# Addition of epsilon to the softmax sums by GpSimd, not by ACT, from the second pair of heads on

## The chip, the cores and the metric

The kernel runs on one core of a Trainium2 chip. The metric is the device time of one execution in microseconds (us). The engines are named as the profile names them: PE (TensorE, matmuls and transposes; PEld its weight loads), DVE (VectorE), ACT (ScalarE), POOL (GpSimd) and SP (the queue that issues most DMAs). Each engine works through its own list of instructions in order, and an instruction that needs another engine's result waits at the head of its list, with all that stand behind it.

## The reference

Two batches of eight heads, 768 tokens, head dimension 64. Attention is allowed between a query and a key that fall to the same of 16 clusters; two dense layers follow, each w_in (512 to 2048) and w_out (2048 to 512), with an activation between.

```
scores = where(mask, q @ k.T / 8, -1e9)
scores = scores - max(scores, axis=-1)
attn = exp(scores)
attn = attn / (sum(attn, axis=-1) + 1e-9)
x = attn @ v                      # (2, 8, 768, 64), laid out as (1536, 512)
x = leaky(x @ w_in) @ w_out
out = rational(x @ w_in2) @ w_out2
```

The change concerns the `+ 1e-9`.

## The kernel before

The attention stage comes first and takes about a third of the time. Its work is cut into 96 **units**: 128 queries of one head against all 768 keys. Twelve units make a **head pair** (two heads), and there are eight head pairs. Two successive units, an even and an odd one, share one small tile `sum` (128 x 2) for their softmax sums; such a **couple** is normalized together. There are 48 couples. The two dense layers (`make_h`, L1097 for `h` and `y`) follow, and PE works there without a pause.

The order of instructions on each engine is that in which `run` writes them. Its loop over i has one step for each unit:

- DVE: `row_max(i)` (L592, the negated maximum `nm` over the scores of unit i in PSUM); in even steps `recip` (L615, the reciprocal of `sum` of the couple i-2, i-1); further down two subtractions `lo(i-4)` (L646, the low half `pl` of the transposed probabilities in `pT`); then what the preparation of later heads needs (`is_max` L357, `first` L365, `onehot` L372), and `merge_add` (L684, tile `xf`).
- POOL: in even steps `normalize` of the units i-2 and i-1 (L619, `e` times the reciprocal, 128 x 768 each); then `finish` (L702 and L703, which cut an attention result `xf` into a high half `xha`/`xhb` and a low half `xla`/`xlb`); then pieces of preparation in the slot "end": `vsplit` (L447, L448), `split_hi` and `split_lo` (L293, L298), `rank` (L362, which needs the result of `is_max` on DVE). Late in the stage it also cuts the first weights of the dense layer (L920, `wil`, which needs `wih` of ACT, L917).
- ACT: two casts `hi(i-4)` (L640, `ph`), copies for the preparation, `exp(i)` (L603, which also adds up the row into `sum`), and in odd steps `denom(i)` (L610, `sum` plus the constant in `eps`).
- PE: six transposes of unit i-4 (L627, into two `pT` tiles), the scores of unit i+1 (L583, `s`), and the product with the values (L663, `o`).

The PSUM tiles in which the transposes land rotate over three buffers (`pq`), shared with the transposes and similarities of the preparation. So a transpose can start when the tile three places before it has been read, for the most part by the subtraction L646. `denom`, `recip` and `normalize` of one couple are a chain: `exp` of the odd unit, the addition, the reciprocal, the two multiplications.

Of the kernel before, what the change touches and what calls it, by code (L numbers as in the profile page):

```python
# [13 lines left out]
AF = mybir.ActivationFunctionType  # L14
ALU = mybir.AluOpType
# [2 lines left out]

P = 128
BIG = float(2.0 ** 60)  # L20
LN_SHIFT = 63
SQRT_MAGIC = float(0x1FBD1DF5)
EXP_SCALE = 2.0 ** -112
# [7 lines left out]
def clustered_attention_moe_moe2(  # L31
# [14 lines left out]
    nc = tc.nc  # L46
# [30 lines left out]
    for c in range(C):  # L77
        nc.vector.memset(iom[:, :, c:c + 1], float(c - C))
    eps = const.tile([P, 1], F32, name="eps")
    nc.vector.memset(eps, 1e-9)  # L80
    lnb = const.tile([P, 1], F32, name="lnb")
    nc.vector.memset(lnb, -LN_SHIFT * math.log(2.0))
    lnc = const.tile([P, 1], F32, name="lnc")
    nc.vector.memset(lnc, 1.000001 * 2.0 ** -LN_SHIFT)
    av = const.tile([P, 4], F32, name="av")
# [48 lines left out]
    UP = HP * T  # L134
    NU = NPAIR * UP
# [6 lines left out]
    class Attention:  # L142
# [65 lines left out]
        def prep_pieces(self, p):  # L208
# [196 lines left out]
            def onehot_near_out(i, h):  # L405
                x = st["pp"].pop(("n", i))[D:KB, 0:S]
                y = st["b"][D:KB, i, h].rearrange("p t n -> p (t n)")
                if i == 0:
                    nc.scalar.activation(y, x, AF.Copy, scale=-BIG)
                else:  # L410
# [13 lines left out]
            def onehot_out(hs=ALL):  # L424
# [3 lines left out]
                for i in range(2):  # L428
                    nc.scalar.activation(
                        st["ot"][0:C * T, i, hs[0]:hs[1]],  # L430
                        pp[0:C * T, i, hs[0]:hs[1]], AF.Copy, scale=-BIG if i == 0 else 1.0,
                    )
# [171 lines left out]
                un["e"], un["s"][:, 0:S], AF.Exp, bias=un["nm"], accum_out=un["recip"]  # L604
            )

        def denom(self, u, alone=False):
            un = self.unit[u]
            x = un["recip"] if alone else un["sum"]
            nc.scalar.activation(x, x, AF.Identity, bias=eps)  # L610

        def recip(self, u, alone=False):
            un = self.unit[u]
# [162 lines left out]
        def run(self, extra, fill):  # L776
            TL = 4
            pieces = {}
            for p in range(NPAIR):
                for i, slot, f in self.prep_pieces(p):  # L780
                    pieces.setdefault(max(i, -1), {}).setdefault(slot, []).append(f)
            self.startup(*fill)
            first = -1
            last_prep = max(pieces)
            n_groups = NU // QT
            part = -(-2 * T // QT)
            for i in range(first, NU + TL + 11):
                def go(slot):
                    for f in pieces.get(i, {}).get(slot, []):
                        f()  # L790

                gi, r = divmod(i - TL - 3, QT)
                ok = 0 <= gi < n_groups
                live = 0 <= i - TL < NU
                go("dve0")
                if 0 <= i < NU:
                    self.row_max(i)
                if i == 1:
                    f0 = self.pair[0]["fn"]
                    f0["rank"]((1, 2), nc.vector)  # L800
                    f0["first"]((1, 2))
                    f0["onehot"](0, (1, 2))
                    f0["onehot"](1, (1, 2))
                if NU - 1 <= i <= NU:
                    self.recip(i - 1, True)
                    self.normalize(i - 1)
                elif i % 2 == 0 and 0 <= i - 2 < NU:
                    self.recip(i - 2)
                    self.normalize(i - 2)
                    self.normalize(i - 1)  # L810
                if live:
                    self.trans_p(i - TL, 0)
                    self.hi(i - TL, 0)
                    self.trans_p(i - TL, 1)
                    self.hi(i - TL, 1)
                if ok and r == QT - 1:
                    self.values(gi, part * r, 2 * T)
                    self.merge_copy(gi)
                go("act")
                if 0 <= i < NU:  # L820
                    self.exp(i)
                    if i >= NU - 2:
                        self.denom(i, True)
                    elif i % 2 == 1:
                        self.denom(i)
                if 0 <= i + 1 < NU:
                    self.scores(i + 1)
                go("pe")
                if ok and r < QT - 1:
                    self.values(gi, part * r, part * (r + 1))  # L830
                if live:
                    self.lo(i - TL, 0)
                    self.lo(i - TL, 1)
                go("pa")
                if ok and r == QT - 1:
                    self.merge_add(gi)
                go("dve")
                gd, rd = divmod(i - TL - 3 - 7, QT)
                if rd == 0 and 0 <= gd < n_groups:
                    self.finish(gd)  # L840
                go("end")
                if 0 <= i < TL:
                    self.warm(5)
                if i == UP:
                    fill[1].preload(4)
                if UP + 6 <= i < NU - 2 * UP and i % 3 == 0:
                    fill[1].step()
                if i == last_prep:
                    self.pc.close()
                    extra[0]()  # L850
                elif i > last_prep:
                    extra[1](i >= NU + TL)
# [167 lines left out]
    with tc.manual_schedule():  # L1020
# [60 lines left out]

        LNC = float(2.0 ** -LN_SHIFT)
        LAG = 3
# [246 lines left out]
```

## Time and profile before

| what | value |
|---|---|
| median of 3 runs | 793.15 us (792.27 to 793.41) |
| profiled execution, its own time | 793.16 us |
| its span, first to last instruction | 791.0 us |
| PE, PEld busy | 775.6 us (98%), 659.6 us (83%) |
| DVE, ACT, POOL busy | 646.7 us (82%), 510.6 us (65%), 387.7 us (49%) |
| chain that ended last | PE 85%, DVE 7%, ACT 3%, POOL 2% |

The shares are means over stages that differ. The attention stage runs from the start to about 262 us of the span. In it DVE, ACT and POOL are far busier than over the whole, and the small instructions that the change moves all lie in it.

### The profile page before, as it was taken

Reading aid. Unit: us, or ns where it says so; the run is one execution under the profiler, and the core shown is the slowest. Engines: PE = TensorE matmul, PEld = TensorE weight load, DVE = VectorE, ACT = ScalarE, POOL = GpSimd, SP = SyncE. Lnnn points to the kernel's source line nnn. Section 1 sums busy time; section 2 is a strip of 40 time slices with the busy share of each in tenths; the row PEclk is TensorE's granted clock in tenths of the full one; section 3 lists DMA queues with packets and bytes.
Section 4 is the critical chain, followed back from the end, with each engine's and each line's share of the span. In section 5 each row is a group of like instructions: output and inputs, shape, how many; then the busy total and the mean of one; then the engine's idle time right before and its main releaser. Section 6 shows DMA issues by size and latency. Waiting matters only on the chain.

```text
span 791.0 us, 11944 instructions
## 1 busy us (share of the span) xinstructions
PE 775.6 (98%) x4026; PEld 659.6 (83%) x4026; DVE 646.7 (82%) x1106; ACT 510.6 (65%) x1015; POOL 387.7 (49%) x400
## 2 busy tenths in 40 slices
PE   8899999999999999999999999999999999999997
PEld 6699999899878888888888888888888888888886
DVE  7888999998988678877577568759988888888896
ACT  5789998998899455454254346357766666666662
POOL 3787887877576324230031023267645545653341
PEclk9999999999999999999999999999999999999999
DMA  3594563662320334335445453530101001000012
GB/s 103 153 236 122 150 150 86 146 172 65 92 91 1 106 107 149 117 128 213 139 145 179 131 179 112 187 106 28 54 13 41 27 27 41 15 0 1 1 54 106
DMA packets 42109, 78.58 MB, mean 99 GB/s; under 512 B 5248, under 2 KB 25280, under 8 KB 42048
## 3 DMA queue, kind: packets, MB, share of 16 engines
q1 hardware_dynamic: 41760, 77.65, 32.5%
q8 instruction: 32, 0.52, 0.3%
q14 instruction: 29, 0.24, 0.1%
q10 hardware_dynamic: 288, 0.16, 0.1%
HBM read 49.84 MB, written 9.96 MB: 76 GB/s over the span
## 4 chain that ended last, share of the span: by engine, by line
PE 85%; DVE 7%; ACT 3%; POOL 2%; issue 1%; DMA 1%; DVEq 0%; SPq 0%; POOLq 0%; ACTq 0%
PE h L1097 32%; PE y L1097 31%; PE o L663 6%; PE s L583 6%; PE pT L627 6%; PE sims L326 2%; DVE pl L646 2%; DVE nm L592 2%; ACT ph L640 1%; PE pa L243 1%; POOL e L619 1%; ACT e L603 1%; DVE acc L1218 1%; DMA st<-in_moe_w_in_dram 1%; PE warm L722 1%
## 5 line engine op out<-in xcount | busy, mean ns | idle before, releaser
L646 DVE TENSOR_TENSOR pl<-pT,ph 128x384 fp32r<-128x384 f32 x192 | 97.2, 547 | 15.7 <-ACT ph L640 15.5
L619 POOL TENSOR_SCALAR e<-e,sum 128x768 f32<-128x768 f32 x96 | 87.5, 923 | 43.6 <-DVE sum L615 29.0
L920 POOL TENSOR_TENSOR wil<-wf,wih 128x512 fp32r<-128x512 f32 x32 | 42.8, 1350 | 128.3 <-ACT wih L917 116.7
L1130 ACT CAST gh<-h 128x512 fp32r<-128x512 f32 x96 | 56.4, 588 | 69.4 <-DVE h L1177 67.9
L1097 PE MATMUL h<-xha,wil 128*128 128x512 f32 x256 | 99.7, 390 | 0.0
L1097 PE MATMUL h<-xla,wih 128*128 128x512 f32 x256 | 99.7, 389 | 0.0
L1097 PE MATMUL h<-xha,wih 128*128 128x512 f32 x256 | 99.7, 389 | 0.0
L1150 POOL TENSOR_SCALAR z<-y,abv 128x512 f32<-128x512 f32 x48 | 37.0, 771 | 117.3 <-ACT y L1146 117.3
L1135 DVE TENSOR_TENSOR gl<-h,gh 128x512 fp32r<-128x512 f32 x96 | 65.6, 686 | 33.8 <-ACT gh L1130 33.5
L640 ACT CAST ph<-pT 128x384 fp32r<-128x384 f32 x192 | 82.2, 481 | 15.2 <-PE pT L627 13.4
L592 DVE TENSOR_REDUCE nm<-s 128x1 f32<-128x768 f32 x96 | 90.9, 947 | 0.5
L603 ACT ACTIVATE e<-s,nm 128x768 f32<-128x768 f32 x96 | 87.4, 910 | 5.7 <-DVE nm L592 3.5
L627 PE MATMUL pT<-ident,e 128*128 128x128 f32 x576 | 81.0, 275 | 1.9 <-DVE pl L646 1.8
L1218 DVE TENSOR_TENSOR acc<-y,acc 128x512 f32<-128x512 f32 x84 | 56.9, 691 | 29.8 <-PE y L1097 29.5
L910 DVE SCALAR_TENSOR_TENSOR wf<-st,wf 128x512 int32<-128x512 int32 x124 | 80.4, 702 | 0.0
L1097 PE MATMUL y<-gl,woh 128*128 128x512 f32 x192 | 74.9, 390 | 0.2 <-DVE gl L1135 0.2
L1097 PE MATMUL y<-gh,wol 128*128 128x512 f32 x192 | 74.8, 389 | 0.0
L1097 PE MATMUL y<-gh,woh 128*128 128x512 f32 x192 | 74.7, 389 | 0.0
L1097 PE MATMUL y<-woh,gl 128*128 128x512 f32 x191 | 74.5, 390 | 0.0
L1097 PE MATMUL y<-woh,gh 128*128 128x512 f32 x191 | 74.4, 390 | 0.0
L1097 PE MATMUL y<-wol,gh 128*128 128x512 f32 x191 | 74.4, 389 | 0.0
L627 PEld LDWEIGHTS pT<-ident,e 128*128 128x128 f32 x576 | 67.3, 143 | 7.5 <-DVE pl L646 2.1
(130 smaller groups left out, 1904.0 us busy)
## 6 DMA issues: line engine op xcount, KB each, us to landing
st<-in_moe_w_out_dram SPq DMA_DIRECT2D x32, 512.0 KB, 4.5
st<-in_moe_w_in_dram SPq DMA_DIRECT2D x30, 512.0 KB, 4.6
a<-hl SPq DMA_DIRECT2D x56, 192.0 KB, 4.0
b<-hl SPq DMA_DIRECT2D x28, 192.0 KB, 5.4
wf<-scratch_wi SPq DMA_DIRECT2D x14, 256.0 KB, 2.9
qraw<-in_q_dram SPq DMA_DIRECT2D x16, 192.0 KB, 3.3
kraw<-in_k_dram SPq DMA_DIRECT2D x16, 192.0 KB, 3.7
vraw<-in_v_dram SPq DMA_DIRECT2D x8, 384.0 KB, 5.1
```

The lines of the kernel that those rows point to most:

```text
L583: nc.tensor.matmul(s[:, n0:n1], lhsT=x[0:hi, 0, t, :], rhs=kk[:, n0:n1], start=m == 0, stop=m == 1,)
L592: nc.vector.reduce_max(un["nm"], un["s"][:, 0:S], axis=AX.X, negate=True)
L603: nc.scalar.activation(un["e"], un["s"][:, 0:S], AF.Exp, bias=un["nm"], accum_out=un["recip"])
L619: nc.gpsimd.tensor_scalar(un["e"], un["e"], un["recip"], 1.0, op0=ALU.mult, op1=ALU.mult)
L627: nc.tensor.transpose(pp[:, kt * P:(kt + 1) * P], un["e"][:, k0:k0 + P], ident)
L640: nc.scalar.copy(un["hi", part], un["pT", part])
L646: nc.vector.tensor_tensor(self.group[gi]["pl"][:, part * n:(part + 1) * n, i * P:(i + 1) * P], un["pT", part], f32(un["hi", part]), op=ALU ...
L910: nc.vector.scalar_tensor_tensor(wi, hold["st", i][:, :, :, 1 - w], sc, wi, op0=op, op1=ALU.bitwise_or)
L1097: nc.tensor.matmul(o, lhsT=l, rhs=r, start=(first and idx == 0), stop=(last and idx == n - 1),)
L1130: nc.scalar.copy(d["gh"], d["h"])
L1135: nc.vector.tensor_tensor(d["gl"], d["h"], f32(d["gh"]), op=ALU.subtract)
L1218: nc.vector.tensor_tensor(a, y, a, op=ALU.add)
```

## The change

For the couples of units 13 to 93 the addition of epsilon is done by POOL, at the end of the odd step, behind that step's "end" pieces. There are 41 such couples. The six couples of the first head pair keep ACT, as do the last two units, which are handled singly.

```
+EPS = 1e-9
...
-        def denom(self, u, alone=False):
+        def denom(self, u, alone=False, gp=False):
             un = self.unit[u]
             x = un["recip"] if alone else un["sum"]
-            nc.scalar.activation(x, x, AF.Identity, bias=eps)
+            if gp:
+                nc.gpsimd.tensor_scalar(x, x, EPS, 1.0, op0=ALU.add, op1=ALU.mult)
+            else:
+                nc.scalar.activation(x, x, AF.Identity, bias=eps)
...
                     if i >= NU - 2:
                         self.denom(i, True)
-                    elif i % 2 == 1:
+                    elif i % 2 == 1 and i < UP:
                         self.denom(i)
...
                 go("end")
+                if UP <= i < NU - 2 and i % 2 == 1:
+                    self.denom(i, gp=True)
```

Three places show the new order. The line numbers of the changed kernel are a few higher (L612 is the addition on POOL, L619 there the reciprocal, L623 the normalization).

POOL, the two couples at the turn of a head pair, before: `e` is the normalization of two units, `vs` is `vsplit`, `xha`/`xla` is `finish`, `sv` is `rank`.

```order
L619 TENSOR_SCALAR e<-e,sum 128x768 x2
L447 TENSOR_SCALAR vs<-vraw 128x6x64
L448 TENSOR_TENSOR vs<-vraw,vs 128x6x64
L702 TENSOR_SCALAR xha<-xf 128x384
L703 TENSOR_TENSOR xla<-xf,xha 128x384
L619 TENSOR_SCALAR e<-e,sum 128x768 x2
L447 TENSOR_SCALAR vs<-vraw 128x6x64
L448 TENSOR_TENSOR vs<-vraw,vs 128x6x64
L362 TENSOR_TENSOR sv<-sv,iom 128x384
```

The same place in the changed kernel:

```order
L623 TENSOR_SCALAR e<-e,sum 128x768 x2
L448 TENSOR_SCALAR vs<-vraw 128x6x64
L449 TENSOR_TENSOR vs<-vraw,vs 128x6x64
L706 TENSOR_SCALAR xha<-xf 128x384
L707 TENSOR_TENSOR xla<-xf,xha 128x384
L612 TENSOR_SCALAR sum<-sum 128x2
L623 TENSOR_SCALAR e<-e,sum 128x768 x2
L448 TENSOR_SCALAR vs<-vraw 128x6x64
L449 TENSOR_TENSOR vs<-vraw,vs 128x6x64
L363 TENSOR_TENSOR sv<-sv,iom 128x384
L612 TENSOR_SCALAR sum<-sum 128x2
```

The addition stands behind the pieces of the couple before it, and ahead of the normalization.

DVE around `rank`, with the semaphores waited for, before:

```order
L357 TENSOR_TENSOR sv<-sv,mx 128x384 [waits DVE_49]
L592 TENSOR_REDUCE nm<-s 128x1 [waits PE_49]
L615 RECIPROCAL sum<-sum 128x2 [waits Activation_49]
L646 TENSOR_TENSOR pl<-pT,ph 128x3x128 [waits Activation_49] x2
L365 TENSOR_REDUCE mx<-sv 128x24 [waits Pool_49]
```

The same place in the changed kernel:

```order
L358 TENSOR_TENSOR sv<-sv,mx 128x384 [waits DVE_49]
L593 TENSOR_REDUCE nm<-s 128x1 [waits PE_49]
L619 RECIPROCAL sum<-sum 128x2 [waits Pool_49]
L650 TENSOR_TENSOR pl<-pT,ph 128x3x128 [waits Activation_49] x2
L366 TENSOR_REDUCE mx<-sv 128x24 [waits DVE_49]
```

DVE's order stays; its reciprocal now waits for POOL, not for ACT. No other instruction of DVE, PE or SP changes its place.

ACT, the step of an odd unit and the next, before (`x` is a copy for the preparation, `tmp` one for the merge):

```order
L603 ACTIVATE e,sum<-s,nm 128x768
L610 ACTIVATE sum<-sum,eps 128x2
L640 CAST ph<-pT 128x3x128 x2
L246 ACTIVATE x<-pa 128x384
L603 ACTIVATE e,sum<-s,nm 128x768
```

And in the changed kernel:

```order
L604 ACTIVATE e,sum<-s,nm 128x768
L644 CAST ph<-pT 128x3x128 x2
L247 ACTIVATE x<-pa 128x384
L604 ACTIVATE e,sum<-s,nm 128x768
L644 CAST ph<-pT 128x3x128 x2
```

The addition between the exponential and the casts is gone.

## Rows read from the trace of the kernel before

**Rows 1.** Busy time by stretch: us from start, length, each engine, granted clock, DMA share, GB/s.

```profile
150.00:180.00 30.00, 29.82 (x210) 27.43 (x209) 28.93 (x54) 27.29 (x67) 23.92 (x28) 1.00 0.54 143
200.00:222.00 22.00, 21.07 (x139) 18.67 (x137) 20.89 (x40) 19.80 (x47) 13.00 (x17) 1.00 0.26 60
```

**Rows 2.** Chain by line, first for 150 to 180 us, then for 200 to 222 us.

```profile
by line: PE o L663 28.4%; PE pT L627 27.1%; PE s L583 26.3%; PE sims L326 8.4%; PE pa L243 4.4%; ACT ph L640 2.9%; PE po L418 1.6%; ACT sv L337 0.8%; issue 0.3%
...
by line: DVE pl L646 33.1%; DVE nm L592 30.7%; POOL e L619 8.1%; issue 5.9%; DVE xf L684 5.4%; DVE sv L357 3.6%; POOL xla L703 3.4%; DVE oh L372 2.8%; DVE sum L615 2.2%; POOL xlb L703 2.1%; DVE mx L365 2.1%; POOL xha L702 1.7%; POOL xhb L70
```

**Rows 3.** Line L610: ns min/median/max, and who waited for it (us, times).

```profile
L610 ACT ACTIVATE sum<-sum,eps x49: 294/296/298, 20.4 to 255.4; 128x2 f32<-128x2 f32 x47, 128x1 f32<-128x1 f32 x2
...
  DVE sum L615: 1.3, 3
```

**Rows 4.** Timeline of POOL (start us, length us), two small instructions.

```profile
0.24 0.10 POOL L1314 MEMSET const-float32-0.0<- 128x1 f32 x1 [0.24 <-issue]
...
192.13 0.30 POOL L702 TENSOR_SCALAR xhb<-xf 128x128 fp32r<-128x128 f32 x1
```

**Rows 5.** The page's group of the normalization: busy us, mean ns, idle before it, releaser.

```profile
L619 POOL TENSOR_SCALAR e<-e,sum 128x768 f32<-128x768 f32 x96 | 87.5, 923 | 43.6 <-DVE sum L615 29.0
```

**Rows 6.** Timelines of POOL and DVE: the last `finish` before five reciprocals, and these.

```profile
78.96 1.01 POOL L703 TENSOR_TENSOR xla<-xf,xha 128x384 fp32r<-128x384 f32 x1
79.95 0.15 DVE L615 RECIPROCAL sum<-sum 128x2 f32<-128x2 f32 x1
...
108.98 1.01 POOL L703 TENSOR_TENSOR xla<-xf,xha 128x384 fp32r<-128x384 f32 x1
109.63 0.16 DVE L615 RECIPROCAL sum<-sum 128x2 f32<-128x2 f32 x1
...
139.07 1.01 POOL L703 TENSOR_TENSOR xla<-xf,xha 128x384 fp32r<-128x384 f32 x1
139.31 0.15 DVE L615 RECIPROCAL sum<-sum 128x2 f32<-128x2 f32 x1
...
169.12 1.02 POOL L703 TENSOR_TENSOR xla<-xf,xha 128x384 fp32r<-128x384 f32 x1
169.39 0.16 DVE L615 RECIPROCAL sum<-sum 128x2 f32<-128x2 f32 x1
...
198.61 1.01 POOL L703 TENSOR_TENSOR xlb<-xf,xhb 128x384 fp32r<-128x384 f32 x1
199.43 0.16 DVE L615 RECIPROCAL sum<-sum 128x2 f32<-128x2 f32 x1
```

**Rows 7.** Timeline around one `rank`, the reciprocal and the normalization behind it.

```profile
203.63 1.01 POOL L362 TENSOR_TENSOR sv<-sv,iom 128x384 f32<-128x384 f32 x1 [0.49 <-DVE sv L357]
...
204.34 0.15 DVE L615 RECIPROCAL sum<-sum 128x2 f32<-128x2 f32 x1
...
204.66 1.79 POOL L619 TENSOR_SCALAR e<-e,sum 128x768 f32<-128x768 f32 x2
```

**Rows 8.** Timelines of DVE and PE: two subtractions, and transposes into the buffer they free.

```profile
179.71 1.00 DVE L646 TENSOR_TENSOR pl<-pT,ph 128x384 fp32r<-128x384 f32 x2
...
180.76 0.55 PE L627 MATMUL pT<-ident,e 128*128 128x128 f32 x3
```

**Rows 9.** Timeline of 224 to 247 us, late in the attention stage.

```profile
227.19 0.15 DVE L615 RECIPROCAL sum<-sum 128x2 f32<-128x2 f32 x1
...
227.79 1.01 POOL L703 TENSOR_TENSOR xlb<-xf,xhb 128x384 fp32r<-128x384 f32 x1
...
228.84 0.55 DVE L684 TENSOR_TENSOR xf<-o,tmp 64x384 f32<-64x384 f32 x1 [0.51 <-POOL xlb L703]
...
232.18 0.62 ACT L917 CAST wih<-wf 128x512 fp32r<-128x512 f32 x1 [0.52 <-POOL vs L448]
```

**Rows 10.** Chain that ended last, 222 to 262 us: start us, length us, what.

```profile
237.32 0.30 ACT sum L610
```

More of the change, by code (lines that the diff above doesn't have):

```diff
@@ L79, in clustered_attention_moe_moe2 @@
     eps = const.tile([P, 1], F32, name="eps")
-    nc.vector.memset(eps, 1e-9)
+    nc.vector.memset(eps, EPS)
     lnb = const.tile([P, 1], F32, name="lnb")
```

## The prediction

> **What bounds the kernel now.** I read the chain that ended last first, then busy time by stretch, then the timelines of the couples. In the middle of the attention stage the chain by line is PE's for some 95%: values, transposes, scores, similarities [rows 2]. ACT has about 4% of it and DVE nothing. PE is busy for 29.82 of 30 us there, but the reader should look at the next column too: DVE is busy for 28.93 of the same 30 us, POOL only for 23.92 and ACT for 27.29 [rows 1]. So PE is the bound and DVE is an almost equal second, with 1.07 us to spare in a whole head pair (one takes 169.39 - 139.31 = 30.1 us, from one reciprocal to the same one of the next head pair [rows 6]). Later the order is reversed: between 200 and 222 us the chain is DVE's subtractions and maxima, with POOL's normalization and its `finish` behind them [rows 1, 2]. The dense layers behind the stage hold PE without a pause, so what the attention stage loses or gains arrives at the end unchanged.
>
> How close DVE stands to PE shows in the PSUM tiles: one pair of subtractions ends at 179.71 + 1.00 = 180.71 us, and the transposes into the tile that it frees start at 180.76 us [rows 8]. That is 0.05 us of room. A DVE that falls behind in this stretch stops PE almost at once.
>
> **What the change removes.** 41 additions leave ACT, 0.296 us each [rows 3], together 12.1 us of ACT's time. In the PE-bound part they lie beside PE's work and are worth nothing. DVE waited for one of the 49 only three times, 1.3 us in all [rows 3]: the addition on ACT was nearly always ready before the reciprocal wanted it. In the late part, from 222 us on, one addition lies on the chain between an exponential and a cast of weights, 0.30 us [rows 10]. I credit **-0.30 us** for it, and as a bound ten couples from 205 us on, -3.0 us.
>
> **What it adds to POOL.** The trace has no POOL instruction on 128 x 2 values. The nearest rows are a memset of 128 x 1 at 0.10 us and a one-input scalar operation on 128 x 128 at 0.30 us [rows 4]; these are my two bounds. From 128 to 768 columns the same kind of operation grows from 0.30 to 0.923 us [rows 4, 5], 0.00097 us a column, which leaves 0.30 - 0.125 = 0.175 us beside the columns. I take 0.20 us, an estimate from these rows, nearest the line through them. Behind it comes the way from POOL to DVE: `finish` ends at 227.79 + 1.01 = 228.80 us and DVE's `xf` that waits for it starts at 228.84 us [rows 9], 0.04 us. So the reciprocal can start 0.24 us after POOL is free.
>
> The Trainium skill, page "GPSIMD Engine Reference", section "Elementwise — side-by-side cycle accounting", would make the fixed part smaller: it gives 4497 ns for an addition of 2048 elements at about 2.6 cycles each and a clock of 1.2 GHz, which leaves about 0.06 us, an estimate from that page. No run so far shows it, and the rows above speak for more. By 0.06 us the twelve waits below would shrink by 12 x 0.14 = 1.7 us, and the sum would be 798.0 us.
>
> **The wait that it adds.** The time of the instruction matters less than its place. It stands on POOL behind the pieces of the odd step, and DVE's reciprocal now waits for it. Behind the reciprocal, on the same in-order engine, stand the two subtractions that free PSUM tiles for PE and the next maximum, for which ACT's exponential waits. POOL's idle time before the normalization is 43.6 us over the stage, 29.0 of it ended by the reciprocal [rows 5]: in most couples POOL is early, it reaches the addition before the exponential ends, and then 0.20 us on POOL in place of 0.296 us on ACT does no harm. What counts are the couples in which POOL is still at its pieces when DVE reaches the reciprocal. There are three kinds.
>
> First, `finish` behind `vsplit`. In five couples, one in each head pair but the first, POOL ends `finish` after the reciprocal began: by 79.97 - 79.95 = 0.02 us, 109.99 - 109.63 = 0.36, 140.08 - 139.31 = 0.77, 170.14 - 169.39 = 0.75 and 199.62 - 199.43 = 0.19 us [rows 6]. That is 2.09 us; with 5 x 0.24 it makes **3.29 us** of waiting on DVE.
>
> Second, `rank`. It is released by DVE itself, by the instruction two places ahead of the reciprocal, and ends at 203.63 + 1.01 = 204.64 us, 0.30 us after the reciprocal began at 204.34 [rows 7]. Since both hang on DVE, this wait comes on top of any delay before it: 0.30 + 0.24 = 0.54 us. `rank` stands in front of one moved addition in each of six head pairs: 6 x 0.54 = **3.24 us**.
>
> Of both kinds PE has 0.05 us of room [rows 8] in each of the five head pairs in which PE leads, **-0.25 us**; in the last one DVE itself is the chain. DVE cannot make up the rest within the dense stretch between the two waits and the tight tile, since its spare 1.07 us lie elsewhere in the head pair.
>
> Third, one couple near the end: the reciprocal began at 227.19 us, `finish` ends at 228.80 us [rows 9], so it comes 1.61 + 0.24 = 1.85 us late. But DVE stood 0.51 us for that same `finish` anyway, and a little later ACT's cast of the weights waits for `vsplit` on POOL at 232.18 us [rows 9], so the chain goes over POOL. POOL falls behind by the addition and the round trip to DVE and back: 0.20 + 0.04 + 0.15 (the reciprocal) + 0.17 (from its end at 204.49 to the normalization at 204.66 us [rows 7]) = **0.56 us**. I take that, with 1.85 us as the upper bound. The later weights cut by L920 stand behind the addition in the new order, so they don't delay it.
>
> Four or five other couples are late by less than POOL's instruction itself, or stand where PE has far more room than 0.05 us; I count nothing for them, up to +0.6 us in the range.
>
> **Sum.** 3.29 + 3.24 - 0.25 + 0.56 - 0.30 = 6.54 us. The profiled execution took 793.16 us by its own time, 0.01 us from the median of the runs shown, 793.15; with the sum it is 799.7 us. Slower by 0.8%. With 0.10 us for the instruction the twelve waits give 1.2 us less, with 0.30 us as much more. If PE has half a microsecond more room in the early head pairs and ACT's relief counts in five more late couples (-1.5), the low end is 6.54 - 1.2 - 0.5 - 1.5 = 3.3 us, 796.5 us; with 1.85 for 0.56 and the small couples the high end is 6.54 + 1.2 + 1.3 + 0.6 = 9.6 us, and I end the forecast's own range at 802.5.
>
> **The rivals.**
>
> *The waits are hidden.* If DVE's lateness is made up before PE needs the tiles, nothing is left but the credit: 792.9 to 793.2 us. For it: three buffers rotate, and between 150 and 180 us the chain has no DVE at all [rows 2]. Against it: the 0.05 us of room, and 28.93 of 30 us busy [rows 1, 8]. It needs room of more than 1.5 us behind the worst head pair (0.77 + 0.24 + 0.54).
>
> *Faster by ACT's relief.* From 205 us on PE doesn't lead; if ACT's queue sets the pitch of the last ten couples, each gains 0.30 us: 793.2 - 3.0 = 790.2 us. For it: the addition on the chain at 237.32 us [rows 10]. Against it: between 200 and 222 us DVE and POOL fill the chain and ACT does not appear [rows 2]. It decides only if less than 3 us of the waits above reach PE.
>
> *POOL becomes the bound of the loop.* Normalization, pieces, addition, reciprocal and back to the normalization is now one circle. In the couples of rows 6 POOL had no pause before, so there the circle grows by the 0.56 us of a round trip. If this lag carries over from couple to couple, all bounds are at their upper ends: 6.54 + 1.2 + 1.3 + 0.6 + 0.3 (no credit) = 9.9 us, 803.1 us. Against it: over a head pair POOL has 30 - 23.92 = 6.1 us to spare [rows 1], and six round trips of 0.56 us take 3.4.
>
> **How the numbers follow.** About 0.2% (1.6 us) is what a measurement of this kernel can tell from no change. The forecast, 796.5 to 802.5 us, gets 0.60; hidden, within 0.2%, 0.15; faster 0.12; POOL's loop above 802.5 us 0.08; a small loss between 794.8 and 796.5 us 0.05. Slower then has 0.60 + 0.08 + 0.05 = 0.73, same 0.15, faster 0.12. A range of 792.0 to 802.5 us leaves out the loop (0.08) and nearly all of faster (0.11): 0.81 inside.
>
> **What would show it.** Right: DVE's reciprocal waits for POOL's `sum` some 12 times, about 6 to 8 us in all; POOL's instruction takes near 0.2 us; the pitch of a head pair in the middle of the stage grows from 30 us by 0.8 to 1.5 us; PE's transposes wait for the subtractions there; and PE works on the dense layers at its old pace. Wrong: a pitch of 30.0 us with the same waits of DVE (hidden), a shorter stretch from 200 to 262 us (ACT's relief), or POOL's idle time before the normalization gone altogether (the loop). The prediction fails if the room behind DVE is larger than the one tile that I measured says, or if POOL, starting its pieces at another time, is no longer late.

## The result and the profile after

The changed kernel takes 799.8 us (median of 5 runs, 799.29 to 801.71); the kernel before, beside it, 792.27 us (791.7 to 793.41). The ratio is 1.0098, 95% interval 1.0083 to 1.0112: slower by 1.0%, about 7.5 us. A second timing in a later set of runs (below) gave 1.0107.

Couples are numbered from 0 here, couple k being units 2k and 2k+1; the change moves the additions of couples 6 to 46.

The profiled execution took 801.71 us, with a span of 799.9 us, 8.9 us more than before. The page: first the chain that ended last by engine, then the group of the normalization, which answers to [rows 5].

```profile
PE 77%; DVE 10%; POOL 7%; ACT 3%; issue 2%; DMA 1%; DVEq 0%; POOLq 0%; SPq 0%; ACTq 0%
...
L623 POOL TENSOR_SCALAR e<-e,sum 128x768 f32<-128x768 f32 x96 | 87.6, 923 | 26.9 <-DVE sum L619 22.9
```

PE's share of the chain fell from 85 to 77%, and POOL, which had 2%, has 7%. POOL's idle time before the normalization fell from 43.6 to 26.9 us; it is not gone.

Busy time by stretch, for the two stretches of [rows 1] (columns as there):

```profile
150.00:180.00 30.00, 28.58 (x199) 25.86 (x198) 27.17 (x53) 24.71 (x58) 24.40 (x33) 1.00 0.43 112
200.00:222.00 22.00, 20.98 (x139) 18.73 (x138) 20.14 (x38) 17.50 (x40) 14.15 (x21) 1.00 0.41 98
```

In the first, PE had 0.18 us of idle time in 30 us and now has 1.42. DVE went down as well, from 28.93 to 27.17 us: the second-busiest engine did not take over, it waits too. The chain by line in the same 150 to 180 us, which answers to the first line of [rows 2]:

```profile
by line: POOL e L623 15.6%; DVE pl L650 13.1%; issue 12.6%; DVE nm L593 11.3%; POOL xla L707 6.8%; DVE xst L916 5.4%; PE pT L631 5.0%; DVE xf L688 3.5%; POOL vs L449 3.4%; POOL sv L363 3.4%; POOL hl L294 3.4%; POOL xha L706 3.3%; POOL hl L2
```

Here it was PE for some 96% before. Now it runs from POOL to DVE and back, and no engine is busy throughout (PE for 28.58 of 30 us).

The new instruction, by its line: ns min/median/max, when, and who waited for it (us, times).

```profile
L612 POOL TENSOR_SCALAR sum<-sum x41: 191/191/536, 54.6 to 260.0; 128x2 f32<-128x2 f32 x41
...
  DVE sum L619: 11.8, 13
```

DVE's reciprocal waits for it 13 times (waits of 0.13 us, in couples 14, 20, 26 and 32, are not counted among these), 11.8 us in all, where it waited 1.3 us for ACT before [rows 3]. Behind DVE stands PE. The waits of PE for the subtractions (us, times, longest), after:

```profile
PE pT L631 <- DVE pl L650: 8.1, 15, 1.2
```

and before:

```profile
PE pT L627 <- DVE pl L646: 1.8, 4, 0.7
```

The timelines of the changed kernel show where the 13 are. Columns: start us, length us, what, and in brackets the idle time before it and its releaser. From the top these are couple 8, couples 11, 17, 23 (with its `finish`) and 29, couple 30 with its `rank`, couple 35, and couple 41.

```profile
65.51 0.83 POOL L294 TENSOR_SCALAR hl<-x 128x768 fp32r<-128x768 f32 x1 [2.48 <-ACT tmp L680]
66.42 0.19 POOL L612 TENSOR_SCALAR sum<-sum 128x2 f32<-128x2 f32 x1
66.65 0.17 DVE L619 RECIPROCAL sum<-sum 128x2 f32<-128x2 f32 x1 [2.45 <-POOL sum L612]
67.41 0.45 PE L631 MATMUL pT<-ident,e 128*128 128x128 f32 x1 [1.17 <-DVE pl L650]
...
82.40 0.17 DVE L619 RECIPROCAL sum<-sum 128x2 f32<-128x2 f32 x1 [0.25 <-POOL sum L612]
...
113.47 0.17 DVE L619 RECIPROCAL sum<-sum 128x2 f32<-128x2 f32 x1 [0.62 <-POOL sum L612]
...
143.74 1.01 POOL L707 TENSOR_TENSOR xla<-xf,xha 128x384 fp32r<-128x384 f32 x1
144.84 0.19 POOL L612 TENSOR_SCALAR sum<-sum 128x2 f32<-128x2 f32 x1
145.06 0.17 DVE L619 RECIPROCAL sum<-sum 128x2 f32<-128x2 f32 x1 [1.17 <-POOL sum L612]
...
176.67 0.17 DVE L619 RECIPROCAL sum<-sum 128x2 f32<-128x2 f32 x1 [1.20 <-POOL sum L612]
...
180.86 1.01 POOL L363 TENSOR_TENSOR sv<-sv,iom 128x384 f32<-128x384 f32 x1 [0.50 <-DVE sv L358]
181.96 0.19 POOL L612 TENSOR_SCALAR sum<-sum 128x2 f32<-128x2 f32 x1
182.19 0.17 DVE L619 RECIPROCAL sum<-sum 128x2 f32<-128x2 f32 x1 [0.54 <-POOL sum L612]
...
207.38 0.17 DVE L619 RECIPROCAL sum<-sum 128x2 f32<-128x2 f32 x1 [0.29 <-POOL sum L612]
...
236.38 1.00 POOL L707 TENSOR_TENSOR xlb<-xf,xhb 128x384 fp32r<-128x384 f32 x1
237.46 0.19 POOL L612 TENSOR_SCALAR sum<-sum 128x2 f32<-128x2 f32 x1
237.68 0.17 DVE L619 RECIPROCAL sum<-sum 128x2 f32<-128x2 f32 x1 [1.84 <-POOL sum L612]
...
241.41 0.62 ACT L923 CAST wih<-wf 128x512 fp32r<-128x512 f32 x1 [0.24 <-POOL vs L449]
```

The five reciprocals of [rows 6] (79.95, 109.63, 139.31, 169.39, 199.43 us) now stand at 82.40, 113.47, 145.06, 176.67 and 207.38: later by 2.45, 3.84, 5.75, 7.28 and 7.95 us. ACT's cast of [rows 9] is later by 241.41 - 232.18 = 9.23 us, and the end of the span by 8.9. So the loss is built up piece by piece between 60 and 241 us, and the dense layers pass it on as it is.

### The profile page after: what moved, and what is told of

Read it like the earlier page. It is cut to its first block, busy times and chain, and to the rows that moved or that the text cites. A ratio compares the mean times of both kernels' runs of the same rounds, so it can differ in the third digit from the quotient of the medians.

```text
span 799.9 us, 11933 instructions
## 1 busy us (share of the span) xinstructions
PE 779.3 (97%) x4026; PEld 659.9 (82%) x4026; DVE 647.1 (81%) x1106; ACT 502.2 (63%) x974; POOL 396.7 (50%) x441
## 4 chain that ended last, share of the span: by engine, by line
PE 77%; DVE 10%; POOL 7%; ACT 3%; issue 2%; DMA 1%; DVEq 0%; POOLq 0%; SPq 0%; ACTq 0%
PE h L1103 31%; PE y L1103 31%; PE pT L631 4%; PE o L667 4%; PE s L584 4%; DVE pl L650 3%; DVE nm L593 2%; POOL e L623 2%; PE sims L327 2%; POOL xla L707 1%; DVE xf L688 1%; ACT e L604 1%; PE pa L244 1%; ACT ph L644 1%; DVE acc L1224 1%
## 5 line engine op out<-in xcount | busy, mean ns | idle before, releaser
L623 POOL TENSOR_SCALAR e<-e,sum 128x768 f32<-128x768 f32 x96 | 87.6, 923 | 26.9 <-DVE sum L619 22.9
L631 PE MATMUL pT<-ident,e 128*128 128x128 f32 x576 | 84.3, 278 | 8.7 <-DVE pl L650 8.1
```

What stands on the lines that cost most here:

```text
L623: nc.gpsimd.tensor_scalar(un["e"], un["e"], un["recip"], 1.0, op0=ALU.mult, op1=ALU.mult)
L631: nc.tensor.transpose(pp[:, kt * P:(kt + 1) * P], un["e"][:, k0:k0 + P], ident)
```

## The experiments

Three theories stood against each other. **A**, that of the prediction: it is the place that costs, in the couples where POOL is still at its pieces when DVE reaches the reciprocal. There are 13 of these by the waits: 8 (`split_hi`), 11, 17, 23, 29 and 35 (`finish`), 6, 12, 18, 24, 30 and 36 (`rank`) and 41 (`finish`). **B**: every moved addition costs about the same, because POOL has one more instruction and one more hand-over in each couple. **C**: the loss comes from ACT, whose exponentials and casts come at other times without the addition. Times are medians, and the time named second is that of the kernel before in the same set of runs. Ratios are to that kernel, with 95% intervals; they are worked out from the single times and are not the quotient of the two medians. A difference in us behind a ratio is the ratio's. Edits are against the changed kernel.

**The 13 back on ACT, 28 stay on POOL.**

```
-                    elif i % 2 == 1 and i < UP:
+                    elif i % 2 == 1 and not (i >= UP and i // 2 not in LATE):
...
-                if UP <= i < NU - 2 and i % 2 == 1:
+                if UP <= i < NU - 2 and i % 2 == 1 and i // 2 not in LATE:
```

`LATE` stands for the 13 numbers above.

> POOL keeps the addition in 28 couples; ACT has it back in the 13 in which POOL was still at its pieces (or at a wait of theirs) when DVE came to the reciprocal. Theory A (the place: only those 13 cost): no loss is left, 791.5 to 793.0 us beside 792.3 for the kernel before, and DVE's wait for POOL's sum under 1 us in all. Theory B (POOL's added work and round trips, wherever they stand): 28/41 of the 7.5 us stay, about 797.4 us.

Measured: 793.26 us against 792.58, ratio 1.0 (0.9988 to 1.0011). The waits of DVE for POOL's addition in this kernel:

```profile
DVE sum L619 <- POOL sum L612: 1.7, 3, 0.8
```

28 additions on POOL cost nothing that can be measured, 0.9 us at the most by the interval; B wanted some 5 us. B falls. The waits are over the 1 us that was expected: three couples that are not late in the changed kernel (9, 19 and 42) are late here.

**Only the 13 on POOL, the other 28 on ACT.** The same two lines, with `in LATE` on the POOL side and the rest on ACT.

> The reverse: POOL has the addition in the 13 late couples alone, ACT in the other 28. Theory A: nearly the whole loss, 799 to 800 us, DVE waiting for POOL some 11 to 12 us. Theory B: 13/41 of 7.5 us, about 794.7 us.

Measured: 802.19 us, ratio 1.0119 (1.0105 to 1.0132), at least the whole loss with a third of the additions. Its waits:

```profile
DVE sum L619 <- POOL sum L612: 11.5, 13, 2.1
```

**No addition at all in the 41 couples.** The addition of epsilon is left out there, so that neither engine does it.

```
-                if UP <= i < NU - 2 and i % 2 == 1:
-                    self.denom(i, gp=True)
```

> The 41 additions are left out altogether, so the reciprocal takes the plain sum: ACT's relief without any wait for POOL. Theory A with a credit of 0.3 us: 791.5 to 792.5 us. If ACT's relief counts in all of the last ten couples: 789.3 us. Theory C (the loss comes from the changed phase of ACT, not from POOL): slower than before, up to 799 us.

Measured: 792.44 us, ratio 0.9993 (0.9977 to 1.001). Taking the work from ACT does no harm, so C falls, and the time shows no help either (what the trace shows of it stands below, under ACT's credit). Between 200 and 222 us ACT's load is not what sets the pace: there DVE is the fullest engine of this kernel (ACT, the fourth number, has 18.59 of 22 us, with 19.80 in [rows 1]):

```profile
200.00:222.00 22.00, 21.24 (x140) 18.91 (x138) 21.59 (x42) 18.59 (x43) 12.90 (x15) 1.00 0.29 72
```

**All 41 on POOL, but ahead of the step's pieces.** The two lines above go, and behind the exponential stands

```
-                    elif i % 2 == 1 and i < UP:
-                        self.denom(i)
+                    elif i % 2 == 1:
+                        self.denom(i, gp=i >= UP)
```

> All 41 additions stay on POOL, but stand ahead of the pieces of their step, not behind them. Theory A: DVE's waits for POOL's sum nearly vanish (under 3 us); POOL now idles before the pieces, so these and the normalization come later, which PE should have room for: 792 to 795 us. Theory B: as the change, 799 to 800 us.

Measured: 794.6 us, ratio 1.0022 (1.0013 to 1.0031). Four fifths of the loss are gone with the same instructions on the same engine. What is left has another shape, by the waits of this kernel (those for `sum` a little over the 3 us expected):

```profile
DVE sum L619 <- POOL sum L612: 3.2, 9, 0.7
...
DVE xf L688 <- POOL xla L707: 3.6, 7, 1.0
```

Now the pieces stand behind an addition that waits for the exponential, and `merge_add` (`xf`) waits for the late `finish`. That this wait is what the remaining 0.2% consists of was not tested.

**One kind of late couple at a time.** In each, only the couples named have the addition on POOL, at the place of the change; all others are on ACT as before. The edit is the condition, here for `finish`:

```
-                if UP <= i < NU - 2 and i % 2 == 1:
+                if i % 2 == 1 and i // 2 in (11, 17, 23, 29, 35):
```

`finish`, couples 11, 17, 23, 29, 35:

> POOL has the addition in five couples alone, those behind finish in five head pairs (11, 17, 23, 29, 35); ACT in all others. Theory A, the first term of the sum alone: 3.29 - 0.2 = +3.0 us, 795.3 us. Theory B: 5/41 of 7.5, 793.2 us.

Measured: 796.38 us against 792.94, ratio 1.0042 (1.0026 to 1.0058), 3.3 us. Its waits:

```profile
DVE sum L619 <- POOL sum L612: 3.6, 5, 1.0
```

`rank`, couples 6, 12, 18, 24, 30, 36:

> POOL has the addition in six couples alone, those behind rank (6, 12, 18, 24, 30, 36). Theory A, the second term alone: 3.24 - 0.25 = +3.0 us, 795.3 us. Theory B: 6/41 of 7.5, 793.4 us.

Measured: 796.38 us against 792.94, ratio 1.0039 (1.0026 to 1.0052), 3.1 us. Its waits:

```profile
DVE sum L619 <- POOL sum L612: 4.7, 6, 1.3
```

`split_hi`, couple 8 alone, for which the prediction counted nothing:

> POOL has the addition in couple 8 alone, which stands behind split_hi, which waits for a DMA to free its buffer. The prediction counted nothing for it (PE has more than 1 us of room there): 792.3 to 792.8 us. If the 2.45 us that DVE waited there in the changed kernel reach PE: 793.5 to 794.7 us.

Measured: 793.7 us against 792.94, ratio 1.002 (1.0002 to 1.0039), 1.6 us with a wide interval (0.2 to 3.1 us); the medians are 0.8 us apart. The single times go from 792.55 to 797.68 us, and the profiled one, 792.82 us, lost nothing although it has this wait of 1.5 us:

```profile
DVE sum L619 <- POOL sum L612: 1.5, 1, 1.5
```

Couple 41 alone:

> POOL has the addition in couple 41 alone. The third term of the sum alone: +0.56 us, 793.2 us; with nothing absorbed +1.85 us, 794.5 us.

Measured: 793.95 us against 792.54, ratio 1.0021 (1.0012 to 1.003), 1.7 us. Its wait:

```profile
DVE sum L619 <- POOL sum L612: 1.9, 1, 1.9
```

The couples 14, 20, 26 and 32, which are late by less than POOL's instruction:

> POOL has the addition in the four couples alone in which DVE waited 0.13 us for POOL's sum (14, 20, 26, 32). Counted as nothing in the prediction: 792.3 to 792.7 us. If each 0.13 us reaches PE: +0.5 us.

Measured: 791.79 us, ratio 0.9988 (0.9979 to 0.9997). Alone they cost nothing. The 0.12% on the fast side is less than a measurement of this kernel tells from no change, and the first experiment, which has these four and 24 more on POOL, stands at 1.0.

The four kinds that cost add up to 0.42 + 0.39 + 0.20 + 0.21 = 1.22%, with the small four at -0.12% to 1.10%. The change itself, once more beside the last two:

> The change itself, unaltered, beside the others on one chip: +7.5 us on the kernel before, 799 to 801 us, DVE waiting for POOL's sum 11 to 12 us.

Measured: 801.02 us against 792.54, ratio 1.0107 (1.0093 to 1.0121). So the kinds add up to the whole, within their intervals. Its waits, a little under those expected:

```profile
DVE sum L619 <- POOL sum L612: 10.8, 14, 1.9
```

**The addition on POOL twice.** Behind POOL's addition stands a second one of 0.0, so that every one of the 41 couples has two such instructions.

```
                 if UP <= i < NU - 2 and i % 2 == 1:
                     self.denom(i, gp=True)
+                    un = self.unit[i]
+                    nc.gpsimd.tensor_scalar(un["sum"], un["sum"], 0.0, 1.0, op0=ALU.add, op1=ALU.mult)
```

> All 41 on POOL as in the change, each followed by a second addition of 0.0 on the same tile, 0.19 us more on POOL ahead of the reciprocal. Theory A: only the 13 late couples see it, 13 x 0.19 = +2.5 us on the change, 802.3 us. Theory B: all 41 do, 41 x 0.19 = +7.8 us, 807.6 us.

Measured: 805.88 us, ratio 1.0157 (1.0129 to 1.0185), 0.50 to 0.59% above the change (by its two ratios), 4.0 to 4.7 us. This lies between what A and B expected. With the intervals of both ratios it is anything from 1.5 to 7.2 us, so A's 2.5 us is not excluded and B's 7.8 us is. The trace says why A's was too small. Timeline and waits of this kernel (L849 is the second addition):

```profile
119.22 0.19 POOL L612 TENSOR_SCALAR sum<-sum 128x2 f32<-128x2 f32 x1
119.50 0.19 POOL L849 TENSOR_SCALAR sum<-sum 128x2 f32<-128x2 f32 x1
```

```profile
DVE sum L619 <- POOL sum L849: 16.9, 17, 2.1
```

The second starts 0.28 us behind the start of the first, which it depends on, so a late couple loses 0.28 us more, not 0.19. And there are 17 late couples now: with 0.28 us more the four small ones are late as well. 13 x 0.28 = 3.6 us, 17 x 0.28 = 4.8 us, and the measured 4.0 to 4.7 lies between.

**The addition on DVE.** To see how much room DVE has, the additions of the 41 couples go there, ahead of the reciprocal; no POOL wait is left.

```
         def recip(self, u, alone=False):
...
+            if not alone and u >= UP:
+                nc.vector.tensor_scalar(x, x, EPS, None, op0=ALU.add)
```

> The 41 additions are done by DVE, in front of the reciprocal, some 0.15 us each: no wait for POOL, but DVE gets longer. It tests how little room DVE has. If 0.05 us of room in the dense stretch is right, four additions of 0.15 us lie in the stretch of each of five head pairs and five more where DVE leads: about +3.4 us, 795.5 to 796.5 us. If DVE's 1.07 us to spare in a head pair take them up: 792.3 to 793.0 us.

Measured: 798.97 us against 792.54, ratio 1.0081 (1.0067 to 1.0095), 6.4 us, nearly twice what was expected. The new instruction by its line (ns min/median/max), and its group (busy us, mean ns):

```profile
L620 DVE TENSOR_SCALAR sum<-sum x41: 147/158/1131, 54.0 to 257.6; 128x2 f32<-128x2 f32 x41
```

```profile
L620 DVE TENSOR_SCALAR sum<-sum 128x2 f32<-128x2 f32 x41 | 9.5, 232 | 0.2
```

At the median of 0.158 us, 41 of them would be 6.5 us; they took 9.5. Of the work that DVE got, about two thirds reach the end (6.4 of 9.5 us): DVE has little room in this stage.

No version ran faster than the kernel before by more than a measurement tells.

## Why the prediction was right, and where its sum was off

**The step that carried it was right.** The time comes from the place of the instruction behind POOL's pieces, not from POOL's work: 28 additions cost nothing that can be measured, 13 cost at least the whole loss, and moved ahead of the pieces the 41 cost a fifth. The way to PE is the one described, reciprocal, subtraction, transposes: PE's waits for the subtractions rose by 6.3 us.

**POOL's instruction.** 0.20 us was estimated from [rows 4, 5]; it took 0.191. The estimate of 0.06 us worked out from the Trainium skill's page "GPSIMD Engine Reference" does not agree with that row. The way to DVE was counted without one of its parts: the addition starts 0.09 us after the piece before it has ended (143.74 + 1.01 = 144.75, to 144.84), and the reciprocal 0.03 us after the addition (145.03, to 145.06). From POOL's last piece to DVE it is 0.31 us, not 0.24.

**`finish`.** The five waits were forecast as 3.29 us and are 0.25 + 0.62 + 1.17 + 1.20 + 0.29 = 3.53 us. Alone they cost 3.3 us; with its share of the 0.25 us of room the term was 3.0. Right.

**`rank`.** Forecast 3.24 us, 0.54 each. In the changed kernel's profile five of the six wait 0.53 or 0.54 us, but couple 6 waits 1.29; with `rank` alone couples 6 and 12 wait 1.3 us. In these, POOL comes late to `rank` itself and does not stand waiting for DVE: the second `vsplit` instruction ahead of it took 1.20 to 1.38 us, where it takes 1.02 us ahead of couple 6 in the second profile of the changed kernel, with a wait of 0.60 us there. Alone the six cost 3.1 us. Right, and so was the claim that both waits of a head pair add up: from 113.47 us on a head pair takes 31.59, 31.61 and 30.71 us, where [rows 6] give 29.68, 30.08 and 30.04. That is 4.1 us; by the terms it is 1.5 + 1.5 + 1.0.

**Couple 41 and ACT's credit belong together.** Alone, couple 41 costs 1.7 us (0.8 to 2.4), close to the 1.85 us that was named as the upper bound. That does not carry over to the change, as the reciprocals of couples 40 and 44 show, before:

```profile
223.54 0.15 DVE L615 RECIPROCAL sum<-sum 128x2 f32<-128x2 f32 x1
...
242.13 0.15 DVE L615 RECIPROCAL sum<-sum 128x2 f32<-128x2 f32 x1
```

and in the changed kernel:

```profile
232.12 0.15 DVE L619 RECIPROCAL sum<-sum 128x2 f32<-128x2 f32 x1
...
251.03 0.15 DVE L619 RECIPROCAL sum<-sum 128x2 f32<-128x2 f32 x1
```

From the one to the other it is 18.59 us before and 18.91 in the changed kernel (18.94 in its second profile): 0.32 us more, with a wait of 1.84 us in between. The prediction's third term and its credit make 0.56 - 0.30 = 0.26 us. With couple 41 alone on POOL, and the other additions on ACT, it is 19.56 us, 0.97 more. With no addition on either engine it is 18.27 us, 0.32 less, and 0.31 less in the kernel that has the 13 back on ACT; in the four kernels with `finish`, `rank`, couple 8 or the small four alone, where ACT keeps its additions in this stretch, it is within 0.03 us of that before. So ACT's credit is there, though the time of the kernel without additions (0.07% below, interval from -0.23 to +0.10%) can't tell it; that time does exclude the 3 us of the rival. Together the two terms came out as forecast. Apart they did not: couple 41 costs 0.97 us and not 0.56 while ACT keeps its additions, and the relief is then worth 0.97 - 0.32 = 0.65 us behind it and not 0.30.

**Couple 8 was late, and PE had the room.** Nothing was counted for the couples "late by less than POOL's instruction itself", or where PE has room. The timeline of the kernel before has couple 8:

```profile
64.14 0.83 POOL L293 TENSOR_SCALAR hl<-x 128x768 fp32r<-128x768 f32 x1 [1.00 <-ACT sum L610]
...
64.23 0.15 DVE L615 RECIPROCAL sum<-sum 128x2 f32<-128x2 f32 x1
```

By the prediction's own rule that is 64.97 - 64.23 + 0.24 = 0.98 us late, more than POOL's instruction. The room is there too: PE's transposes behind it wait 1.17 us where DVE waited 2.45 in the changed kernel, 0.79 for 2.05 with the 13 alone, 0.30 for 1.56 with the addition twice, 0.10 for 1.37 in the second profile of the change. That is a room of 1.26 to 1.28 us in four profiles, against 0.05 us in the dense stretch; with couple 8 alone PE does not wait there at all, for 1.49 us of DVE. What the prediction left out is that the lateness differs from one execution to the next. POOL's queue stands at semaphores ahead of `split_hi`, at the longest for 3.5 us before and 5.0 us after (ns min/median/max):

```profile
L293 POOLq EVENT_SEMAPHORE  x32: 43/43/3477, 35.0 to 180.2; - x32
...
L294 POOLq EVENT_SEMAPHORE  x32: 42/43/5012, 35.7 to 187.7; - x32
```

By the traces the longest is the one ahead of couple 8, and it ends 0.03 us after a transfer `a<-hl` has landed, at 63.82 us before and at 65.19 in the changed kernel. Where the transfer lands later, DVE is late by more than the room, and PE waits: 1.17 us in the changed kernel's profile, 0.10 in its second. So the 1.6 us of couple 8 alone stand for executions that lost little or nothing, as the profiled one, and others that lost more; how often it is late was not measured.

**So the sum was short.** 6.54 us were forecast, and two timings gave about 7.5 and 8.5 us. The start of the reciprocals shows where the profiles differ from the forecast. The columns give by how much each stretch is longer than before, in us. The forecast has the terms of the couples in it, for the first row 0.54 + 0.26 + 0.54 - 0.05 (couples 6, 11 and 12 and the room), for the last 0.56 - 0.30.

| reciprocals | before | forecast | changed kernel | its second profile | the 13 alone |
|---|---|---|---|---|---|
| up to couple 12 | 84.86 | 1.29 | 3.06 | 2.58 | 2.81 |
| couple 12 to 40 | 138.68 | 4.99 | 5.52 | 5.75 | 5.05 |
| couple 40 to 44 | 18.59 | 0.26 | 0.32 | 0.35 | 1.05 |

With the 13 alone on POOL, the stretch from couple 12 to 40 is longer by almost exactly the forecast, and by what DVE's eight waits there add up to, 5.11 us. With the other 28 on POOL as well, 0.5 to 0.7 us come on top. That lies inside the interval of the run with those 28 alone, and in that run ACT's credit works against it; which of them cost it was not tested. Most of the shortfall lies ahead of couple 12. In the changed kernel's profile the 0.75 us more in couple 6 and the 1.17 us of PE behind couple 8 account for it; in the second profile some 0.8 us stay open. Single executions differ there by as much: the same reciprocal is 1.20 us later than before in the kernel without additions and 0.14 us earlier in that with the small four.

That the prediction of 799.7 us meets the measured 799.8 us so closely is luck in part: the kernel before has a median of 792.27 us in the later runs, 0.9 us below the one from which it was reckoned, and this made up for most of the short sum.

**The rivals.** *Hidden* falls: the waits come through, and the addition on DVE shows that a delay of DVE in this stage is passed on for the most part. *Faster by ACT's relief* falls with the additions left out. *POOL's loop* is half seen: the chain of 150 to 180 us does go round between POOL and DVE with no engine busy throughout. But its price is that of the forecast, some 1.5 us a head pair, and POOL keeps 26.9 us of idle time before the normalization. DVE's waits were given as 6 to 8 us in 12; they are 11.8 in 13, since couples 8 and 41 have 4.3 us of them and couple 6 has 0.75 us more than forecast.

## What to carry to other kernels

An engine's idle share does not tell whether a small instruction can move there. Look at two queues: what stands ahead of it on the new engine at the moment when its result is wanted, and what stands behind the instruction that will wait for it. List all such places, those that occur only once too, and read for each how much room the engine behind has there. Here the waits of the dense stretch arrived in full, 1.27 us of that at couple 8 did not, and of the 1.84 us at couple 41 a sixth did, since the same move took work off the chain there. Where a place hangs on a transfer, give it a range and not a number.

## What the runs showed of the hardware that was not expected

**A tiny instruction can be held for as long as a large one.** In the kernel with the additions on DVE, nine of the 41 took over 0.2 us, the longest 1.131. In each the addition ended within 0.03 us of the end of a POOL instruction that was running. Timelines of POOL and DVE in that kernel:

```profile
109.99 1.02 POOL L709 TENSOR_TENSOR xla<-xf,xha 128x384 fp32r<-128x384 f32 x1
110.13 0.90 DVE L620 TENSOR_SCALAR sum<-sum 128x2 f32<-128x2 f32 x1
```

POOL ends at 111.01 us, DVE's addition on two columns at 111.03. In the changed kernel it goes the other way, in two of the 41:

```profile
138.01 0.67 DVE L916 SCALAR_TENSOR_TENSOR xst<-xst 128x512 int32<-128x512 int32 x1
138.23 0.51 POOL L612 TENSOR_SCALAR sum<-sum 128x2 f32<-128x2 f32 x1 [0.73 <-ACT e L604]
```

DVE ends at 138.68 us, POOL's addition at 138.74 instead of 0.19 us after its start. The Trainium skill, page "SBUF — State Buffer", section "Who interferes with whom", says that DVE and GpSimd share a pair of ports as an exclusive lock, that whoever issues first keeps it for the whole instruction, and that `tensor_scalar` on DVE can be a form that takes it. The first trace agrees with all three, 0.90 us for 0.158; the second with the lock, 0.51 us for 0.191 (DVE's instruction there is no `tensor_scalar`). The nine held additions took 4.5 us where nine at the median take 1.4, which makes up the difference between 9.5 and 6.5 us.

**The clock.** In the profiles of the kernel before and of the change the granted clock falls to 0.50 (1.2 of 2.4 GHz) for some 3 us once in the attention stage, but not at the same place. Before, it is here (columns as in [rows 1]):

```profile
24.90:28.00 3.10, 3.10 (x12) 1.93 (x11) 2.84 (x5) 0.78 (x3) 1.34 (x2) 0.50 0.60 184
```

In the changed kernel's profile it comes after the wait of couple 8:

```profile
64.30:67.00 2.70, 1.94 (x16) 1.74 (x15) 0.35 (x2) 2.03 (x4) 1.04 (x3) 1.00 0.97 230
67.20:70.50 3.30, 3.09 (x15) 2.91 (x15) 3.21 (x7) 2.02 (x5) 3.30 (x4) 0.50 0.24 56
```

PE was busy for 1.94 of 2.70 us ahead of the fall. Since each of these two has one such stretch, it moves the early times against each other and not the end. The wait does not bring the fall there by itself: the second profile of the changed kernel waits 1.37 us at couple 8 and has the fall where the kernel before has it,

```profile
24.90:28.00 3.10, 3.10 (x12) 1.90 (x11) 2.93 (x5) 1.16 (x3) 1.34 (x2) 0.51 0.46 136
```

and the profile with the 13 alone waits 2.05 us there and has no fall in the attention stage. What decides the place stays open.
